# A linear-attention and two-MLP kernel: another order of the second product, weight sums on DVE, later splits for the next tokens, a plain store for the last visit

## The chip, the cores and the metric

The kernel runs on one core of one Trainium2 chip. The metric is the device time of that core in microseconds (us). The kernel before took 1151.75 us, the median of three runs (1151.14 to 1152.44).

The engines are named as in the profile: PE multiplies matrices (PEld is its loading of weights), DVE and ACT do arithmetic and evict PE's accumulators, POOL does arithmetic and issues some DMAs, SP issues most DMAs.

## The reference

```python
kv  = einsum('bhsd,bhse->bhde', k, v)                 # 4 batches, 8 heads, 576 x 64
out = einsum('bhsd,bhde->bhse', q, kv)
x   = out / sqrt(mean(out * out, -1) + 1e-6) * g_norm
x   = x.transpose(0, 2, 1, 3).reshape(2304, 512)
h   = maximum(maximum(x @ w1, x @ w2), x @ w3)        # first MLP, 512 -> 768
x   = h @ w_out                                       # 768 -> 512
p   = domain_probs / (domain_probs.sum(-1) + 1e-9)    # second MLP: 4 experts
for e in range(4):
    h    = maximum(x @ w1[e], 0.0)                    # 512 -> 1024
    out += p[:, e:e+1] * (h @ w2[e])                  # 1024 -> 512
```

All of it is fp32. The change lies in the second MLP, which takes from about 381 us of the span to its end.

## The kernel before

**Numbers and products.** An fp32 operand is split into two fp32r parts, hi and lo: ACT copies the value into hi, which rounds it, and DVE forms lo = value - hi. A product is then three matmuls, hi*hi, lo*hi and hi*lo. On top of that every product of 2x2 blocks is made by seven products of sums of blocks in place of eight products of blocks (Winograd's form of Strassen's method). So a weight matrix goes through three steps before PE can use it: a load by SP, *sums* of its blocks (`w1_sums`, L530, and `w2_sums`, L558, four instructions of 128x256 each, on POOL), and *splits* (`w1_split`, L536 on ACT and L500 on DVE; `w2_split`, L564 and L565), in two halves of 768 and 1024 columns. The tokens y, which are the output of the first MLP, are stored to DRAM as y_d and come back by the same three steps: `y_load`, `y_sum` (L581, four of 128x768, on DVE and POOL in turn) and `y_split` (seven of them, one for each product).

**Visits and units.** The 2304 tokens are three pairs of blocks, sb = 0, 1, 2, of 768 tokens. The hidden columns of the four experts are cut into eight parts, q = 0 to 7 (two for each expert). A visit is one q with one sb; there are 24, in an order in which sb goes 0, 1, 2, then 2, 1, 0, and so on. From visit 0 to 1 and from 1 to 2 the tokens of the next sb are prepared for the first time (**changes of tokens**, the first and the second); their split operands are stored to DRAM by `op_store` and come back ready by `op_load` in all later visits. Each time q advances, at units 6, 12, ... 42, the weights change (**changes of weights**, seven). A visit has two units, r = 0 and 1.

**A unit** is seven slots. In slot k PE makes product k of the first stage (x @ w1 of this visit): six matmuls of 128x384 into bank A or bank X (L604, order AXAXAAX), and then some matmuls of the second stage (h @ w2) of the *previous* visit, 10, 9, 9, 8, 10, 9 and 8 of them, 128x256 each (L855). `after_product` evicts the first stage: product 0 is copied by ACT from bank A into bank X (L658); the additions that read bank X and so free it are on DVE (L645); ReLUs, sums (`relu_sum`, L648; `op_sub`, L694) and splits (`op_hi`, L633 on ACT; `op_lo`, L638 and L640 on DVE) form the operands of the second stage. All but the first steps go through `later(t, ...)`, which puts them into a slot by its number; `at(n, k, ...)` does the same for loads, sums and splits of weights, and `turn_y` for the tokens. Within a slot the order of issue is: product, second stage with its evictions, `later`, `turn_y`, `at`. Each engine works through its own queue in that order.

**The second stage** of a visit is seven products j of 18 matmuls, over three accumulators of two banks each, which rotate from visit to visit. `JACC` gives the accumulator of product j: 0, 2, 1, 0, 2, 0, 0. After product 0 ACT copies accumulator 0 into 1 (L826), so that product 2 adds to it; products 3, 5 and 6 go on in accumulator 0, product 4 in 2. `after_second` evicts products 1, 2, 3, 6 on ACT (L836, scaled by p) and adds products 4 and 5 to them on DVE (L838), each in three instructions. The finished rows of block 0 go out after product 4, those of block 1 after product 6, by `put_out`: a DMA from POOL's queue, which for q > 0 adds to what is in DRAM (`accum_op`). The second stage of the last visit has no unit beside it and stands alone at the end.

## Time and profile before

| | |
|---|---|
| median of three runs | 1151.75 us (1151.14 to 1152.44) |
| the profiled execution | 1152.46 us, its span 1150.7 us |
| mean granted clock of PE | 0.981 |
| PE busy | 1083.1 us, 94% |
| DVE busy | 759.9 us, 66% |
| ACT busy | 595.2 us, 52% |
| POOL busy | 364.8 us, 32% |

A span is what the profiler saw between the first and the last instruction; the time of the execution lies 1.8 us above it. The share of an engine is its busy time by the span, over stages of very different kinds, so the stretches, waits and timelines below are read beside it. "Idle before, releaser" in a row is the time for which the engine stood in front of that work and what it was waiting for at the end.

### The profile page before, as it was taken

The page shows a single profiled execution, that of the slowest core. Times are in us where ns is not written, and L with a number is a line of the kernel's source. Part 1 is how long each engine was busy: PE and PEld are TensorE (multiplying, and loading weights), DVE is VectorE, ACT ScalarE, POOL GpSimd, SP SyncE. Part 2 cuts the span into 40 slices and gives each one's busy share as a digit, 9 for nine tenths or more (in the row PEclk, how much of TensorE's full clock was granted, in tenths as well). Part 3 has the DMA queues.
Part 4 walks back from the last instruction along what each step waited for, and adds up shares of the span by engine and source line. Part 5 has one row for each costly group of instructions (what it writes and reads, how often), then busy time and mean ns, then how long its engine had stood idle before and what let it go on. Part 6 is the DMA issues. An engine that isn't in the chain of part 4 may idle for free.

```text
span 1150.7 us, 19292 instructions
## 1 busy us (share of the span) xinstructions
PE 1083.1 (94%) x7318; PEld 1059.4 (92%) x7318; DVE 759.9 (66%) x1298; ACT 595.2 (52%) x1269; POOL 364.8 (32%) x392
## 2 busy tenths in 40 slices
PE   7889999999999598999999999999999999999995
PEld 6789999999998598999999999999999999999995
DVE  3789985666666866665665675575576476567552
ACT  2543233334344565665565556566556556556553
POOL 1336633420102312512622442341352262253113
PEclk8999999999999898999999999999999999999998
DMA  9945555332412866268668767758858957866855
GB/s 246 295 150 171 154 174 191 128 114 99 133 38 99 312 238 238 93 247 245 131 196 228 173 156 224 208 128 228 237 102 238 282 94 233 231 149 171 230 131 83
DMA packets 109581, 207.61 MB, mean 180 GB/s; under 512 B 13744, under 2 KB 68016, under 8 KB 109488
## 3 DMA queue, kind: packets, MB, share of 16 engines
q1 hardware_dynamic: 88944, 168.29, 43.8%
q0 software_dynamic: 19840, 37.76, 19.1%
q8 instruction: 57, 0.93, 0.3%
q10 hardware_dynamic: 704, 0.33, 0.1%
q14 instruction: 36, 0.29, 0.1%
HBM read 136.35 MB, written 69.99 MB: 179 GB/s over the span
## 4 chain that ended last, share of the span: by engine, by line
PE 49%; DVE 5%; issue 4%; ACT 3%; POOL 1%; POOLq 0%; ACTq 0%; DVEq 0%
PE bank L604 25%; PE bank L855 24%; DVE wl L500 1%; ACT wl L536 1%; DVE ob L838 1%; DVE fa L648 1%; POOL out_dram L813 1%; DVE w2s L838 1%; ACT wr L633 1%; DVE fa L838 1%; ACT fa L836 0%; ACT bank L658 0%; ACT ob L836 0%; DVE fa L645 0%; DVE wr L640 0%
## 5 line engine op out<-in xcount | busy, mean ns | idle before, releaser
L855 PE MATMUL bank<-wr 128*128 128x256 f32 x1683 | 258.5, 284 | 8.9 <-DVE w2s L838 5.1
L855 PEld LDWEIGHTS bank<-wr 128*128 128x128 f32 x1683 | 236.5, 191 | 11.2 <-DVE w2s L838 5.5
L604 PE MATMUL bank<-rb,wl 128*128 128x384 f32 x1032 | 212.0, 341 | 10.6 <-ACT bank L658 10.5
L658 ACT ACTIVATE fa<-bank 128x384 f32<-128x384 f32 x192 | 94.7, 493 | 188.6 <-PE bank L604 181.9
L604 PEld LDWEIGHTS bank<-rb,wl 128*128 128x128 f32 x1032 | 176.6, 189 | 14.1 <-ACT bank L658 12.8
L604 PE MATMUL bank<-xr,wl 128*128 128x384 f32 x864 | 176.4, 339 | 5.9 <-DVE fa L645 4.3
L604 PEld LDWEIGHTS bank<-xr,wl 128*128 128x128 f32 x864 | 146.4, 190 | 7.2 <-DVE fa L645 5.0
L530 POOL TENSOR_TENSOR w1s<-w1s 128x256 f32<-128x256 f32 x96 | 86.8, 924 | 153.3 <-DMA w1s<-in_moe_w_dram 90.5
L640 DVE TENSOR_TENSOR wr<-fa,wr 128x384 fp32r<-128x384 f32 x138 | 83.2, 603 | 56.6 <-ACT wr L633 56.6
L813 POOL DMA_DIRECT2D out_dram<-w2s x49 | 52.3, 1093 | 147.3 <-DVE ob L838 88.5
L855 PE MATMUL bank<-wr,hr 128*128 128x256 f32 x567 | 91.8, 282 | 2.9 <-ACT bank L826 1.4
L813 POOL DMA_DIRECT2D out_dram<-ob x50 | 52.4, 1085 | 128.9 <-DVE fa L838 27.8
L855 PEld LDWEIGHTS bank<-wr,hr 128*128 128x128 f32 x567 | 81.2, 188 | 4.0 <-ACT bank L826 1.6
L633 ACT ACTIVATE wr<-fa 128x384 fp32r<-128x384 f32 x144 | 75.8, 528 | 11.1 <-DVE fa L648 6.6
L813 POOL DMA_DIRECT2D out_dram<-fa x41 | 39.1, 1085 | 106.3 <-DVE fa L838 26.7
L855 PE MATMUL bank<-wr,xr 128*128 128x256 f32 x396 | 68.2, 282 | 1.5 <-DVE w2s L838 1.3
L836 ACT ACTIVATE ob<-bank,p_all 128x256 f32<-128x256 f32 x106 | 50.4, 475 | 30.9 <-PE bank L855 30.9
L645 DVE TENSOR_TENSOR fa<-bank,fa 128x384 f32<-128x384 f32 x96 | 52.9, 551 | 19.6 <-ACT fa L658 17.5
L604 PE MATMUL bank<-op,wl 128*128 128x384 f32 x288 | 60.5, 346 | 5.0 <-ACT fa L658 5.0
L747 DVE TENSOR_TENSOR fa<-bank,fa 128x384 f32<-128x384 f32 x54 | 29.9, 554 | 51.3 <-ACT fa L744 36.0
L836 ACT ACTIVATE w2s<-bank,p_all 128x256 f32<-128x256 f32 x106 | 50.4, 476 | 22.3 <-PE bank L855 22.3
L855 PEld LDWEIGHTS bank<-wr,xr 128*128 128x128 f32 x396 | 58.6, 188 | 2.4 <-DVE w2s L838 1.9
(200 smaller groups left out, 2077.0 us busy)
## 6 DMA issues: line engine op xcount, KB each, us to landing
rb<-op_d SPq DMA_DIRECT2D x42, 768.0 KB, 4.9
xr<-op_d SPq DMA_DIRECT2D x42, 768.0 KB, 9.2
out_dram<-w2s POOLq DMA_DIRECT2D x48, 256.0 KB, 7.7
out_dram<-ob POOLq DMA_DIRECT2D x48, 256.0 KB, 7.1
op<-op_d SPq DMA_DIRECT2D x14, 768.0 KB, 9.7
stage_a<-in_moe_w_dram SPq DMA_DIRECT2D x18, 512.0 KB, 4.1
out_dram<-fa POOLq DMA_DIRECT2D x32, 256.0 KB, 7.9
w1s<-in_moe_w_dram SPq DMA_DIRECT2D x30, 256.0 KB, 3.7
```

Of the source, the lines that this page charges most:

```text
L500: nc.vector.tensor_tensor(out=lo, in0=src, in1=f32(hi), op=ALU.subtract)
L530: eng.tensor_tensor(out=st[o], in0=st[a], in1=st[b], op=ALU.subtract)
L604: nc.tensor.matmul(out, w[wi][:, c * P : (c + 1) * P], y[yi][:, c, :], start=(i == 0 and k in begin), stop=(i == 5), skip_group_check=k no ...
L633: nc.scalar.activation(out=ops[key][0], in_=src, func=AF.Relu if relu else AF.Copy)
L640: nc.vector.tensor_tensor(out=lo, in0=src, in1=f32(hi), op=ALU.subtract)
L645: todo.setdefault(t, []).append(lambda: fn(*args, **kw))
L658: nc.scalar.activation(out=out, in_=in_, func=func)
L747: nc.vector.tensor_tensor(out=mx[done] if i == 0 else t, in0=x, in1=t, op=ALU.add)
L813: nc.gpsimd.dma_start(out=rows, in_=src, accum_op=ALU.add)
L836: nc.scalar.activation(out=o, in_=piece(ps, i), func=AF.Copy, scale=pe)
L838: nc.vector.scalar_tensor_tensor(out=o, in0=piece(ps, i), scalar=pe, in1=o, op0=ALU.mult, op1=ALU.add)
L855: nc.tensor.matmul(piece(ps, i), h[hi][:, i * P : (i + 1) * P], w[wi], start=fresh, stop=last, skip_group_check=True,)
```

## The change

Four things are changed, all in the second MLP:

- The second stage goes through its products in the order 0, 1, 3, 2, 5, 4, 6. The accumulators of `JACC` stay, so that no two products in a row use the same one (0, 2, 0, 1, 0, 2, 0). Product 3 now takes the place of product 2 as the one that opens the rows of block 0.
- All sums of w1, w2 and y are on DVE. They are spread over slots, two instructions in each, and stand in other slots than before. Loads of w2 are called in an earlier slot; on SP's queue they stand in the same place among the other DMAs as before.
- At the two changes of tokens y is summed in slots 0 to 3 and split from slot 3 on (`YLAG`), in place of slots 0 and 1 for the sums and 0 to 6 for the splits. The addition that frees bank X after product 6 is made at once and not through `later`, and the splits of S1, S2 and A12 stand in another order.
- The last visit's rows are loaded back from DRAM into `fa` during the last unit (`get_out`); all its evictions add to them on DVE, and `put_out` stores them plainly from SP's queue.

```diff
--- before.py
+++ after.py
@@ -524,9 +524,9 @@
             src = e_w1[e, :, f * P : (f + 1) * P].rearrange("(c p) f -> p c f", p=P)
             nc.sync.dma_start(out=st[:, at : at + 2].rearrange("p n c f -> p (n c) f"), in_=src)
 
-    def w1_sums(eng, early=False):
+    def w1_sums(eng, early=False, which=(0, 1, 2, 3)):
         st = [t[:, n * 2 * P : (n + 1) * 2 * P] for t in w1_at(early) for n in range(4)]
-        for o, a, b in ((4, 0, 2), (5, 1, 4), (6, 1, 0), (7, 3, 5)):
+        for o, a, b in [((4, 0, 2), (5, 1, 4), (6, 1, 0), (7, 3, 5))[x] for x in which]:
             eng.tensor_tensor(out=st[o], in0=st[a], in1=st[b], op=ALU.subtract)
 
     def w1_split(r, half, early=False):
@@ -551,11 +551,12 @@
                 out=st[:, x : y + 1 : y - x, :], in_=e_w2[e, f * P : (f + 1) * P, :].rearrange("p (n d) -> p n d", n=2)
             )
 
-    def w2_sums(q, r):
+    def w2_sums(q, r, which=(0, 1, 2, 3)):
         t = w2_at(q, r)
         st = [t[:, n * 2 * P : (n + 1) * 2 * P] for n in range(8)]
-        for o, a, b, op in ((1, 7, 0, ALU.subtract), (3, 1, 4, ALU.subtract), (5, 4, 7, ALU.subtract), (6, 2, 3, ALU.add)):
-            nc.gpsimd.tensor_tensor(out=st[o], in0=st[a], in1=st[b], op=op)
+        sums = ((1, 7, 0, ALU.subtract), (3, 1, 4, ALU.subtract), (5, 4, 7, ALU.subtract), (6, 2, 3, ALU.add))
+        for o, a, b, op in [sums[x] for x in which]:
+            nc.vector.tensor_tensor(out=st[o], in0=st[a], in1=st[b], op=op)
 
     def w2_split(q, r, half):
         cols = slice(0, 3 * 2 * P) if half == 0 else slice(3 * 2 * P, 7 * 2 * P)
@@ -676,14 +677,14 @@
             later(t0 + 7, op_hi, key("S1"), u)
             later(t0 + 7, op_lo, key("S1"), u)
             later(t0 + 11, nc.vector.tensor_tensor, out=r21, in0=r11, in1=r21, op=ALU.subtract)
-            later(t0 + 8, op_sub, n, r11, u)
+            later(t0 + 7, op_sub, n, r11, u)
         elif k == 6:
-            later(t0 + 6, nc.vector.tensor_tensor, out=t12, in0=x, in1=t12, op=ALU.add)
+            nc.vector.tensor_tensor(out=t12, in0=x, in1=t12, op=ALU.add)
+            later(t0 + 8, op_hi, key("S2"), u)
             later(t0 + 8, op_hi, key("A12"), t12, True)
+            later(t0 + 9, op_lo, key("S2"), u)
             later(t0 + 9, op_lo, key("A12"), t12, True)
             later(t0 + 10, relu_sum, t12, t12, u, ALU.add)
-            later(t0 + 9, op_hi, key("S2"), u)
-            later(t0 + 10, op_lo, key("S2"), u)
             later(t0 + 11, op_hi, key("S4"), t12)
             later(t0 + 12, op_lo, key("S4"), t12)
             later(t0 + 12, op_hi, key("S3"), r21)
@@ -793,6 +794,7 @@
     ACC = [banks[0:2], banks[2:4], banks[4:6]]
     JOPS = ["A11", "S1", "A12", "S2", "S4", "S3", "A22"]
     JACC = (0, 2, 1, 0, 2, 0, 0)
+    YLAG = 3
     ev_turn = [0]
 
     def new_ev(q):
@@ -804,12 +806,21 @@
     def piece(acc, i):
         return acc[i // 2][:, i % 2 * 2 * P : (i % 2 + 1) * 2 * P]
 
-    def put_out(q, sb, blk, ev, i):
+    def get_out(sb, blk, i):
+        t = (2 * sb + blk) * TPB + i
+        n = P // len(tiles[t])
+        held[blk, i, 1] = part(fa, (blk * TPB + i) * DM, DM)
+        for x, rows in enumerate(tiles[t]):
+            nc.sync.dma_start(out=held[blk, i, 1][x * n : (x + 1) * n, :], in_=rows)
+
+    def put_out(gi, q, sb, blk, ev, i):
         t = (2 * sb + blk) * TPB + i
         n = P // len(tiles[t])
         for x, rows in enumerate(tiles[t]):
             src = ev[x * n : (x + 1) * n, :]
-            if q:
+            if gi + 1 == len(visits):
+                nc.sync.dma_start(out=rows, in_=src)
+            elif q:
                 nc.gpsimd.dma_start(out=rows, in_=src, accum_op=ALU.add)
             else:
                 nc.gpsimd.dma_start(out=rows, in_=src)
@@ -827,22 +838,22 @@
             return
         blk, b = {1: (1, 1), 2: (0, 0), 3: (0, 1), 4: (0, 1), 5: (1, 1), 6: (1, 0)}[j]
         for i in (0, 1) if half == 0 else (2,):
-            if j in (1, 2):
+            if j in (1, 3) and gi + 1 < len(visits):
                 held[blk, i] = new_ev(q)
-            ev = held[blk, i]
+            ev = held[(blk, i) if gi + 1 < len(visits) else (blk, i, 1)]
             pe = p_all[:, (2 * sb + blk) * TPB + i, e : e + 1]
             o = ev[:, b * 2 * P : (b + 1) * 2 * P]
-            if j in (1, 2, 3, 6):
+            if j in (1, 2, 3, 6) and gi + 1 < len(visits):
                 nc.scalar.activation(out=o, in_=piece(ps, i), func=AF.Copy, scale=pe)
             else:
                 nc.vector.scalar_tensor_tensor(out=o, in0=piece(ps, i), scalar=pe, in1=o, op0=ALU.mult, op1=ALU.add)
             if j in (4, 6):
-                put_out(q, sb, blk, ev, i)
+                put_out(gi, q, sb, blk, ev, i)
 
     def second(gi, q, sb):
 
         acc = [ACC[(gi + x) % 3] for x in range(3)]
-        for j in range(7):
+        for j in (0, 1, 3, 2, 5, 4, 6):
             ps = acc[JACC[j]]
             for half, its in enumerate(((0, 1), (2,))):
                 fresh = j in (0, 1)
@@ -1121,45 +1132,45 @@
             at(0, 2 + i, w1_split, 1, i)
             at(0, 5 + i, w2_split, 0, 0, i)
         at(0, 0, w2_load, 0, 0)
-        at(0, 1, w2_sums, 0, 0)
+        at(0, 4, w2_sums, 0, 0)
         at(1, 0, w2_load, 0, 1)
-        at(1, 1, w2_sums, 0, 1)
-        at(1, 5, w2_split, 0, 1, 0)
-        at(2, 1, w2_split, 0, 1, 1)
+        at(1, 5, w2_sums, 0, 1)
+        at(1, 6, w2_split, 0, 1, 0)
+        at(2, 2, w2_split, 0, 1, 1)
         for k in range(7):
             at(0, (0, 1, 2, 3, 5, 5, 5)[k], op_store, 0, k)
-            at(2, k, op_store, 1, k)
-            at(4, k, op_store, 2, k)
+            for sb in range(1, NSB):
+                at(2 * sb - 1, k + YLAG, y_split, k)
+                at(2 * sb, k, op_store, sb, k)
+        for sb in range(1, NSB):
+            for i in range(4):
+                at(2 * sb - 1, i, y_sum, nc.vector, i)
+        at(0, 4, y_load, 1)
+        at(2, 5, y_load, 2)
         for q in range(1, Q):
             e, pr, n = q // 2, q % 2 * 2, 6 * q
             at(n - 2, 0, w1_load, e, pr)
-            at(n - 2, 1, w1_sums, nc.gpsimd)
-            at(n - 1, 1, w1_split, 0, 0)
-            at(n - 1, 3, w1_split, 0, 1)
             at(n - 1, 5, w1_load, e, pr + 1)
-            at(n - 1, 6, w1_sums, nc.gpsimd)
-            at(n, 3, w1_split, 1, 0)
-            at(n, 5, w1_split, 1, 1)
+            for i in range(2):
+                which = (2 * i, 2 * i + 1)
+                at(n - 2, 5 + i, w1_sums, nc.vector, False, which)
+                at(n, 2 + i, w1_sums, nc.vector, False, which)
+                at(n - 1, 1 + 2 * i, w1_split, 0, i)
+                at(n, 4 + i, w1_split, 1, i)
+                for r in range(2):
+                    at(n - 1 + r, 4 + i, w2_sums, q, r, which)
+                    at(n + 1 + i, (0, 3)[r], w2_split, q, r, i)
             for r in range(2):
-                at(n - 1 + r, 4, w2_load, q, r)
-                at(n - 1 + r, 5, w2_sums, q, r)
-                at(n + 1, (0, 3)[r], w2_split, q, r, 0)
-                at(n + 2, (0, 3)[r], w2_split, q, r, 1)
+                at(n - 2 + r, 6, w2_load, q, r)
+        last = len(visits) - 1
+        for blk in range(2):
+            for i in range(TPB):
+                at(2 * last + 1, i, get_out, visits[last][1], blk, i)
 
         def turn_y(gi, r, k):
 
             (q, sb), (_, nxt) = visits[gi], visits[gi + 1]
-            if sb == nxt:
-                return
-            if q == 0:
-                if r == 0 and k == (4 if gi == 0 else 1):
-                    y_load(nxt)
-                if r == 1 and k < 2:
-                    for i in range(2):
-                        y_sum(nc.gpsimd if i else nc.vector, 2 * k + i)
-                if r == 1:
-                    y_split(k)
-            elif r == 1:
+            if q and r == 1 and sb != nxt:
                 op_load(nxt, k)
 
         fill = second_of(*units[-1][:2])
```

PE at the end of a second stage (here that of the last visit; bank4_70 and bank5_71 are accumulator 0, bank2_68 and bank3_69 accumulator 2; wr_957 holds the weights and the other names the operands). Before, products 4, 5 and 6:

```order
L855 MATMUL bank2_68<-wr_957 128x256 x6
L855 MATMUL bank2_68<-wr_957,xr_81 128x256 x6
L855 MATMUL bank3_69<-wr_957 128x256 x3
L855 MATMUL bank3_69<-wr_957,xr_81 128x256 x3
L855 MATMUL bank4_70<-wr_957,xr_81 128x256 x6
L855 MATMUL bank4_70<-wr_957,rb_1097 128x256 x6
L855 MATMUL bank5_71<-wr_957,xr_81 128x256 x3
L855 MATMUL bank5_71<-wr_957,rb_1097 128x256 x3
L855 MATMUL bank4_70<-wr_957 128x256 x6
L855 MATMUL bank4_70<-wr_957,hr_82 128x256 x6
L855 MATMUL bank5_71<-wr_957 128x256 x3
L855 MATMUL bank5_71<-wr_957,hr_82 128x256 x3
```

and now products 5, 4 and 6:

```order
L866 MATMUL bank4_70<-wr_957 128x256 x6
L866 MATMUL bank4_70<-wr_957,xr_81 128x256 x6
L866 MATMUL bank5_71<-wr_957 128x256 x3
L866 MATMUL bank5_71<-wr_957,xr_81 128x256 x3
L866 MATMUL bank2_68<-wr_957,rb_1097 128x256 x6
L866 MATMUL bank2_68<-wr_957 128x256 x6
L866 MATMUL bank3_69<-wr_957,rb_1097 128x256 x3
L866 MATMUL bank3_69<-wr_957 128x256 x3
L866 MATMUL bank4_70<-wr_957 128x256 x12
L866 MATMUL bank5_71<-wr_957 128x256 x6
```

Products 5 and 6, which stood one behind the other on accumulator 0, now have product 4 between them.

DVE at the first change of tokens, in unit 1 (L581, now L582, are sums of y, L694/L695 is `op_sub`, L500 with rb or xr a split of y, L645/L646 with bank6 an addition that frees bank X, L638 to L641 are splits of the second stage's operands, L559 are sums of w2). Before:

```order
L581 TENSOR_TENSOR fa_80<-fa_80 128x768
L500 TENSOR_TENSOR rb_1097<-fa_80,rb_1097 128x768
L694 TENSOR_TENSOR fa_80<-fa_80 128x384
L581 TENSOR_TENSOR fa_80<-fa_80 128x768
L500 TENSOR_TENSOR rb_1097<-fa_80,rb_1097 128x768
L638 SCALAR_TENSOR_TENSOR wr_957<-fa_80,wr_957 128x384
L640 TENSOR_TENSOR wr_957<-fa_80,wr_957 128x384
L500 TENSOR_TENSOR rb_1097<-fa_80,rb_1097 128x768
L648 SCALAR_TENSOR_TENSOR fa_80<-fa_80 128x384
L640 TENSOR_TENSOR wr_957<-fa_80,wr_957 128x384
L500 TENSOR_TENSOR xr_81<-fa_80,xr_81 128x768
L645 TENSOR_TENSOR fa_80<-fa_80 128x384
```

and now:

```order
L695 TENSOR_TENSOR fa_80<-fa_80 128x384
L582 TENSOR_TENSOR fa_80<-fa_80 128x768 x2
L641 TENSOR_TENSOR wr_957<-fa_80,wr_957 128x384
L639 SCALAR_TENSOR_TENSOR wr_957<-fa_80,wr_957 128x384
L641 TENSOR_TENSOR wr_957<-fa_80,wr_957 128x384
L582 TENSOR_TENSOR fa_80<-fa_80 128x768
L649 SCALAR_TENSOR_TENSOR fa_80<-fa_80 128x384
L582 TENSOR_TENSOR fa_80<-fa_80 128x768
L500 TENSOR_TENSOR rb_1097<-fa_80,rb_1097 128x768
L646 TENSOR_TENSOR fa_80<-fa_80 128x384
L646 TENSOR_TENSOR fa_80<-bank6_72,fa_80 128x384
L500 TENSOR_TENSOR rb_1097<-fa_80,rb_1097 128x768
```

All four sums of y stand on DVE, and the first split of y comes behind them, next to the addition that frees bank X and not six instructions ahead of it.

DVE at the second change of weights, in unit 12 (L500 with w1s is a split of w1, L559 with fa are sums of w2). Before:

```order
L500 TENSOR_TENSOR wl_83<-w1s_1626,wl_83 128x768
L645 TENSOR_TENSOR fa_80<-fa_80 128x384
L645 TENSOR_TENSOR fa_80<-bank6_72,fa_80 128x384
L640 TENSOR_TENSOR wr_957<-fa_80,wr_957 128x384
L500 TENSOR_TENSOR wl_83<-w1s_1626,wl_83 128x1024
L640 TENSOR_TENSOR wl_83<-fa_80,wl_83 128x384
L648 SCALAR_TENSOR_TENSOR fa_80<-fa_80 128x384
L645 TENSOR_TENSOR fa_80<-bank6_72,fa_80 128x384
```

and now:

```order
L646 TENSOR_TENSOR fa_80<-fa_80 128x384
L646 TENSOR_TENSOR fa_80<-bank6_72,fa_80 128x384
L500 TENSOR_TENSOR wl_83<-w1s_1626,wl_83 128x768
L559 TENSOR_TENSOR fa_80<-fa_80 128x256 x2
L641 TENSOR_TENSOR xr_81<-fa_80,xr_81 128x384
L500 TENSOR_TENSOR wl_83<-w1s_1626,wl_83 128x1024
L559 TENSOR_TENSOR fa_80<-fa_80 128x256 x2
L682 TENSOR_TENSOR fa_80<-bank6_72,fa_80 128x384
```

The addition that frees bank X (bank6_72, L646) now stands ahead of the split of 768 columns; two pairs of sums came in, and L682, the addition after product 6, stands directly behind the second pair.

## Rows read from the trace of the kernel before

**Rows 1.** Busy time by stretch: length, PE, PEld, DVE, ACT, POOL, granted clock, DMA, GB/s.

```profile
395.00:408.00 13.00, 8.47 (x30) 7.87 (x31) 12.75 (x18) 5.85 (x11) 4.17 (x5) 0.52 0.43 142
...
436.00:443.00 7.00, 6.75 (x30) 6.75 (x31) 5.22 (x10) 2.15 (x5) 0.00 (x0) 0.60 0.87 353
...
462.00:1122.00 660.00, 643.44 (x4484) 637.31 (x4483) 418.38 (x745) 384.37 (x862) 221.53 (x251) 1.00 0.70 190
```

**Rows 2.** Waits of PE from 462 to 1141 us: us in total, times, longest.

```profile
PE bank L604 <- ACT bank L658: 7.3, 7, 1.3
...
PE bank L855 <- DVE w2s L838: 3.6, 8, 0.8
...
PE bank L855 <- DVE ob L838: 3.1, 8, 0.8
...
PE bank L855 <- DVE fa L838: 2.8, 7, 0.8
...
PE bank L855 <- ACT bank L826: 1.4, 1, 1.4
```

**Rows 3.** Timeline of PE, changes of tokens: start, us, work, idle before, releaser.

```profile
395.23 2.29 PE L604 MATMUL bank<-op,wl 128*128 128x384 f32 x6 [4.97 <-ACT fa L658]
...
401.82 2.29 PE L604 MATMUL bank<-xr,wl 128*128 128x384 f32 x6 [4.30 <-DVE fa L645]
...
408.11 1.22 PE L604 MATMUL bank<-rb,wl 128*128 128x384 f32 x6
...
436.25 0.58 PE L855 MATMUL bank<-wr 128*128 128x256 f32 x1 [4.79 <-DVE w2s L838]
```

**Rows 4.** Timeline of DVE and POOL, first change of tokens.

```profile
387.80 0.96 DVE L581 TENSOR_TENSOR fa<-fa 128x768 f32<-128x768 f32 x1 [2.38 <-DMA fa<-y_d]
...
389.54 2.17 DVE L694 TENSOR_TENSOR fa<-fa 128x384 f32<-128x384 f32 x1
...
393.38 2.16 DVE L638 SCALAR_TENSOR_TENSOR wr<-fa,wr 128x384 fp32r<-128x384 f32 x1
...
395.46 1.10 DVE L640 TENSOR_TENSOR wr<-fa,wr 128x384 fp32r<-128x384 f32 x1
...
399.88 0.95 DVE L500 TENSOR_TENSOR xr<-fa,xr 128x768 fp32r<-128x768 f32 x1
...
401.22 0.55 DVE L645 TENSOR_TENSOR fa<-bank,fa 128x384 f32<-128x384 f32 x1
...
388.89 2.41 POOL L581 TENSOR_TENSOR fa<-fa 128x768 f32<-128x768 f32 x1 [21.98 <-ACT fa L658]
...
395.41 4.13 POOL L558 TENSOR_TENSOR ob<-ob 128x256 f32<-128x256 f32 x4 [0.29 <-DMA ob<-in_moe_w_dram]
```

**Rows 5.** Timeline of DVE and PE at the second change of weights.

```profile
581.91 1.23 DVE L500 TENSOR_TENSOR wl<-w1s,wl 128x1024 fp32r<-128x1024 f32 x1 [2.29 <-ACT wl L536]
...
583.99 0.55 DVE L645 TENSOR_TENSOR fa<-bank,fa 128x384 f32<-128x384 f32 x1
...
585.16 1.32 PE L604 MATMUL bank<-rb,wl 128*128 128x384 f32 x6 [0.95 <-ACT bank L658]
```

**Rows 6.** Timeline of POOL and ACT, two units earlier.

```profile
550.70 3.45 POOL L530 TENSOR_TENSOR w1s<-w1s 128x256 f32<-128x256 f32 x4 [7.28 <-DMA w1s<-in_moe_w_dram]
...
552.19 0.47 ACT L658 ACTIVATE bank<-bank 128x384 f32<-128x384 f32 x1 [1.68 <-DVE hr L638]
```

**Rows 7.** Timeline of PE and POOL at the end.

```profile
1139.43 0.52 PE L855 MATMUL bank<-wr,hr 128*128 128x256 f32 x3
...
1144.20 0.90 POOL L813 DMA_DIRECT2D out_dram<-fa  x1 [0.46 <-issue]
```

**Rows 8.** Groups by line, DVE: busy us, mean ns, idle before, releaser.

```profile
L838 DVE SCALAR_TENSOR_TENSOR w2s<-bank,p_all,w2s 128x256 f32<-128x256 f32 x53 | 25.3, 477 | 9.9 <-PE bank L855 9.8
```

**Rows 9.** DMA issues from 360 to 445 us: count, KB each, median us to landing.

```profile
y_d<-fa SPq DMA_DIRECT2D x6, 192.0 KB, 3.5
...
y_d<-ob SPq DMA_DIRECT2D x2, 192.0 KB, 1.9
```

## Prediction

> **What bounds the kernel now.** I read the table of stretches first, then PE's waits, then the timelines at the places where PE stood. From 462 to 1122 us PE is busy 643.4 of 660 us at the full clock of 2.4 GHz [rows 1]: that stage is 97.5% full, and only the missing 16.6 us are to be had there. Outside it two places are poor. At the first change of tokens (visit 0 to 1) PE stood 4.97 and 4.30 us, and from 395 to 408 us the granted clock was 0.52, the 1.2 GHz level; at the second (visit 1 to 2) it stood 4.79 us, and the clock of the next 7 us was 0.60 [rows 1, 3]. At the end the last matmuls finish by 1139.95 us, while the span goes on to 1150.7 us for POOL's last accumulating stores [rows 7].
>
> What PE waited for in the full stage and the tail is in its list of waits. DVE's evictions of the second product (L838) come to 3.6 + 3.1 + 2.8 = 9.5 us in 23 waits [rows 2], one for each visit, since product 6 writes the banks that product 5 has just filled; the 4.79 us are one more of them. ACT's copy of bank A into bank X (L658) is 7.3 us in 7 waits [rows 2], one at each change of weights, as at 585.16 [rows 5].
>
> **The change, part by part.**
>
> *Order of the second product.* Between products 5 and 6 now stands product 4, on other banks: 18 matmuls and at least one product of the next visit's first stage, 24 matmuls of 0.143 us on average (643.4 us by 4484) [rows 1], 3.4 us. In that time DVE has three evictions of 0.477 us to do [rows 8]. So the 23 waits go: **-9.5 us**. No pair in the new order is closer than one that was there already: product 3 follows product 1 and needs ACT's copy of product 0, which product 2 needed at the same place; product 5 has one product between it and product 3, as before. Block 0 is stored one product later, on POOL, for which nobody waits.
>
> *Sums on DVE.* 56 sums of w1 and 64 of w2, each 128x256, go from POOL to DVE. The trace has none on DVE. Undisturbed, a 128x768 and a 128x384 instruction take 1.34 us from 399.88 to 401.22 [rows 4]; I count 0.87 and 0.47 (their 0.95 and 0.55 less the 0.08 that lies under the next), so 1.04 ns a column and 0.34 us for 256. 120 x 0.34 = 41 us go onto DVE; 112 of them lie in the stretch where DVE is busy 418 of 660 us [rows 1], which becomes 456, 69%. They are spread two by two over slots of 15 matmuls, 2.1 us, so what counts is who is queued behind them. **Bank X.** Before, between the split of the weights (ends 583.14) and the addition that frees bank X (583.99) stand two instructions [rows 5]; now two sums stand there (0.68 us) and the addition comes first behind them: it starts 0.2 to 0.3 us earlier, and PE's wait of 0.95 us shrinks by as much. Seven times: **-2 us**. Bounds: the waits go wholly (-7), or a sum costs as much as on POOL, 1.03 us [rows 4], and the wait grows by 1.1 us at each change (+8). I take the value from DVE's own rows.
>
> *The wait that is new.* The sums of w1 wait for their load, now on DVE. At the second change of weights the load landed at 550.70, as POOL's start shows, and the copy that PE waits for ran at 552.19 [rows 6]. Behind the waiting sums stands the addition for bank X: 550.70 + 0.68 + 0.55 = 551.93, so 0.26 us are left. SP's order there is as before, and its transfers too, so I take the landing as it is: **+1 us** over the six changes where POOL waited so, for loads that land a little later against a faster PE; bounds 0 and +6 (each landing 1.3 us later).
>
> *First change of tokens.* DVE's instructions there were held up by POOL: two of 384 columns took 2.17 and 2.16 us where an undisturbed one takes 0.55, and four from 395.46 to 399.88 took 4.42 us instead of 2.28, 5.4 us in all, while POOL did two sums of y (2.41 us the first) and four of w2 [rows 4]. Those six now cost DVE 2 x 0.87 + 4 x 0.34 = 3.1 us. Second, y_split is put off by three slots, so that ACT and DVE come to the instructions that free banks A and X before most of the splits. I count DVE's new order from 387.80 on, where it still waits for the load of y: eleven instructions up to the addition that frees bank X make 7.2 us, so product 6 starts at about 395.0 and not at 401.8, with one stop of some 5 us in place of 4.97 + 4.30; eleven more up to the first split of w2's second half make 5.9 us, and that half is ready at 401. The second product of visit 0 needs it after six matmuls, so product 1 of the next unit starts near 401.3 where it started at 408.11 [rows 3]: 6.8 us. A stop of 5 us left the clock at its lower level before, so I give back 2: **-5 us**, bounds -2 and -9. The Trainium skill ("SBUF — State Buffer", Who interferes with whom) has DVE instructions with two SBUF inputs and GpSimd instructions that read SBUF lock each other out for whole instructions. By that rule this term would be -8 (rival E); the rows agree in kind, but the four sums of 4.13 us cost DVE only 2.1.
>
> *Second change of tokens.* The 4.79 us are the pair 5 and 6, which is gone; the clock's 7 us at 0.60 cost 2.8. DVE's work in that unit, 13 instructions of 0.47, six evictions of 0.4, four sums of y and four splits of 0.87, is about 15.5 us, as long as the 7 slots of 2.1 us that PE takes for it; I allow 0.5 us: **-7 us**, bounds -3 and -7.6.
>
> *The end.* The last visit's outputs come back by SP during the last unit, into a part of fa that nothing uses any more; DVE adds to them from PSUM, three evictions for each product of 18 matmuls (1.4 against 2.6 us). After the last matmul (1139.95, less 0.3 for the pair 5 and 6) come an eviction of 0.48 [rows 8], 0.6 us that I allow for hand-over and issue, and a plain store of 256 KB. No such store is in the trace; stores of 192 KB to y_d landed in 1.9 and 3.5 us [rows 9]. I take 2.7: end near 1143.5 in place of 1150.7, **-7 us**, bounds -5 and -8. The splits of S2, A12 and S3 in another order cost nothing: each is issued at least one slot ahead of its use.
>
> **Sum**: -9.5 - 2 + 1 - 5 - 7 - 7 = -29.5 us. The profiled execution took 1152.46 us (span 1150.7); that gives 1123. It lies 0.7 us above the median of the runs, so 1122 to 1123 for a median; I say **1123**.
>
> **The rivals.** *B, DVE becomes the bound where it was already late.* At the first change of tokens DVE has no idle time from 387.80 on [rows 4]; all sums now stand in its one queue, so the first change may gain nothing, the second only part. With the first at 0, the second at -3 and bank X at 0: -9.5 + 1 - 3 - 7 = -18.5, 1134. Against it: the 5.4 us that POOL took are more than the 3.1 that it hands over. The Trainium skill ("Trace Analysis", Optimizing Scalar/DVE Operations) speaks against the change here: work may be moved off a saturated DVE to Scalar or GpSimd; it adds that GpSimd and DVE share a port, so that it might not help. *C, the pair's wait moves.* In the tail PE waited 1.4 us for ACT's copy of product 0 (L826) [rows 2]. If product 3, now behind product 1, waited 0.5 us for it in each of 23 visits, the order would gain nothing: 1123 + 12 = 1135. For it: the copy must now be past its reading. Against it: product 2 needed the copy at the same place, and the list has that wait once. *D, slower.* DVE stands still for a w1 load that lands late at six changes; each us beyond the 0.26 us of slack costs PE one. The point is a landing 5.3 us later ((5.3 - 0.26) x 6 = 30); 6 us later gives 1123 - 1 + 34 = 1156. For it: 0.26 us is little, and POOL had waited 7.28 us there [rows 6]. Against it: the transfers ahead are the same. *E, better.* POOL's sums held DVE up for as long as they ran, 2 x 2.4 + 4.1 = 9 us [rows 4], and bank X is free in time: -9.5 - 7 + 1 - 8 - 7.6 - 7 = -38, 1114.
>
> **How the numbers follow.** Forecast 0.62, B 0.17, C 0.07, E 0.09, D 0.05. Forecast, B and C lie between 1116 and 1138 with their bounds; leaving out D, half of E and the far ends gives 1113 to 1138. A measurement of this kernel tells about 0.2% (2.3 us) from no change. Faster is all but D and mixtures of D with the rest: 0.92; same 0.03, slower 0.05.
>
> **What would show it.** In the profile after: no wait of PE for an eviction in each visit; PE's waits for ACT's copy at the changes of weights between 0.5 and 0.8 us; sums of 128x256 on DVE near 0.42 us long; product 6 at the first change of tokens near 395 and one stop in place of two; the second stop gone with its low clock; the span's end within 4 us of the last matmul. DVE idle before w1 sums with PE waiting behind it would show D; stops of PE behind DVE from 385 to 440 us as long as before, B. What would most easily make it wrong is the first change of tokens, where I counted a queue by hand.

## The result, and the profile after

| | before | after |
|---|---|---|
| median | 1151.45 us (4 runs) | 1130.76 us (1130.14 to 1131.67, 4 runs) |
| profiled execution, its span | 1152.46 us, 1150.7 us | 1131.67 us, 1129.9 us |
| DVE busy | 759.9 us, 66% | 768.4 us, 68% |
| POOL busy | 364.8 us, 32% | 236.1 us, 21% |

The ratio of the times is 0.9821, with a 95% interval of 0.9804 to 0.9838: 20.7 us less. The prediction said 1123, 28.8 us below the 1151.75 that were known then, and 1113 to 1138. The direction and the range hold; somewhat over a quarter of the forecast gain is missing. The stretches of [rows 1] in the changed kernel (same columns):

```profile
395.00:408.00 13.00, 11.91 (x79) 11.65 (x78) 11.10 (x20) 10.65 (x20) 0.00 (x0) 0.96 0.75 291
436.00:443.00 7.00, 7.00 (x52) 7.00 (x51) 5.86 (x11) 5.01 (x12) 0.00 (x0) 1.00 1.01 387
462.00:1122.00 660.00, 643.39 (x4506) 639.13 (x4505) 425.76 (x851) 382.44 (x858) 119.51 (x141) 1.00 0.71 190
```

The two poor stretches at the changes of tokens are nearly full. The windows lie at the same times and hold later work than before, though: the one long stop that is left at the first change ends at 392.17 us, ahead of the first of them. By the marks explained below, the granted clock went from 0.82 to 0.90 over the first change and from 0.85 to 1.00 over the second. In the full stage PE is busy no longer than it was, 643.39 against 643.44 of 660 us, and makes only 22 matmuls more in that time, about 3 us of work. Its list of waits from 462 us on (us in total, times, longest) says why; it answers to [rows 2]:

```profile
PE bank L866 <- DVE wr L566: 6.1, 7, 0.9
PE bank L605 <- ACT bank L659: 5.4, 7, 1.0
PE bank L605 <- DVE fa L646: 3.0, 6, 0.5
PE bank L866 <- ACT bank L837: 2.1, 1, 2.1
```

The 23 waits for DVE's evictions, 9.5 us, are gone. Two kinds of wait stand there that were not there before: for DVE's split of w2 (L566), once for each change of weights, and for the addition that frees bank X after product 4 (L646), once in the unit ahead of each.

**Where the time went, by stages.** Each unit has exactly one copy of bank A into bank X, which ACT makes after product 0. The starts of these copies are marks by which two traces can be laid side by side; the difference of two marks is the length of a unit, or of several.

| from mark to mark | before | after | gain | forecast |
|---|---|---|---|---|
| start to unit 1 | 383.12 | 380.10 | 3.0 | 0 |
| units 1 and 2 (first change of tokens) | 38.84 | 34.39 | 4.5 | 5 |
| unit 3 (second change of tokens) | 22.77 | 16.70 | 6.1 | 7 |
| units 4 to 46 | 663.73 | 660.64 | 3.1 | 10.5 |
| unit 47 to the end of the span | 42.24 | 38.07 | 4.2 | 7 |

The 3.0 us at the start don't belong to the change. The run with only the new order, whose code up to there is that of before, reached the mark at 381.50. The profiled execution of before had a granted clock of 0.63 from 367 to 371 us; from mark 0 to mark 1 it took 17.61 us, every other kernel of this study 16.04 to 16.09, with the first sums of w2 on either engine. The other 1.4 us are in mark 0 itself, which lies anywhere from 363.55 to 365.74 us in the kernels of this study. So what failed is above all the term of units 4 to 46, and there the unit two behind each change of weights tells most, in which the second product meets the new weights for the first time. Marks of units 14 and 15 before:

```profile
599.69 0.47 ACT L658 ACTIVATE bank<-bank 128x384 f32<-128x384 f32 x1
614.60 0.47 ACT L658 ACTIVATE bank<-bank 128x384 f32<-128x384 f32 x1 [1.68 <-PE bank L604]
```

and after:

```profile
584.40 0.47 ACT L659 ACTIVATE bank<-bank 128x384 f32<-128x384 f32 x1 [0.15 <-PE bank L605]
600.49 0.47 ACT L659 ACTIVATE bank<-bank 128x384 f32<-128x384 f32 x1 [1.66 <-PE bank L605]
```

14.91 us became 16.09, and likewise behind each of the seven changes of weights. The timeline of that unit in the changed kernel:

```profile
591.90 0.48 ACT L847 ACTIVATE w2s<-bank,p_all 128x256 f32<-128x256 f32 x1
592.26 1.07 ACT L565 ACTIVATE wr<-fa 128x1024 fp32r<-128x1024 f32 x1
...
593.36 1.23 DVE L566 TENSOR_TENSOR wr<-fa,wr 128x1024 fp32r<-128x1024 f32 x1 [2.63 <-ACT wr L565]
...
594.64 0.63 PE L866 MATMUL bank<-wr,wl 128*128 128x256 f32 x3 [0.87 <-DVE wr L566]
```

ACT's and DVE's split of the second half of w2 (products 3 to 6) for the second unit stand in slot 3, behind ACT's evictions of product 1. The old order needed that half after 54 matmuls, the new one takes product 3 after 36, and PE stands until the split is made.

### The profile page after: what moved, and what is told of

It reads as the page before. It is cut to its first block, busy times and chain, and to the rows that moved or that the text cites. A ratio compares the mean times of both kernels' runs of the same rounds, so it can differ in the third digit from the quotient of the medians.

```text
span 1129.9 us, 19220 instructions
## 1 busy us (share of the span) xinstructions
PE 1078.0 (95%) x7318; PEld 1056.9 (94%) x7318; DVE 768.4 (68%) x1434; ACT 591.7 (52%) x1257; POOL 236.1 (21%) x261
## 4 chain that ended last, share of the span: by engine, by line
PE 59%; DVE 16%; DMA 8%; issue 7%; ACT 7%; SPq 1%; POOL 1%; DVEq 0%; ACTq 0%; POOLq 0%
PE bank L605 33%; PE bank L866 21%; PE bank L772 4%; DMA w_da<-cv_a 1%; PE bank L424 1%; DMA w1s<-in_moe_w_dram 1%; DMA y_d<-fa 1%; DMA out_dram<-ob 1%; DMA out_dram<-w2s 1%; DVE wr L566 1%; DVE wl L500 1%; ACT wl L536 1%; ACT ob L847 1%; DVE rb L500 1%; DVE cv_a L233 1%
## 5 line engine op out<-in xcount | busy, mean ns | idle before, releaser
L866 PE MATMUL bank<-wr 128*128 128x256 f32 x1701 | 263.6, 283 | 5.0 <-DVE wr L566 2.8
L866 PEld LDWEIGHTS bank<-wr 128*128 128x128 f32 x1701 | 239.5, 190 | 5.8 <-DVE wr L566 3.4
L641 DVE TENSOR_TENSOR wr<-fa,wr 128x384 fp32r<-128x384 f32 x131 | 72.3, 552 | 47.8 <-ACT wr L634 47.6
L824 POOL DMA_DIRECT2D out_dram<-w2s x48 | 48.5, 1037 | 200.1 <-DVE ob L849 152.0
L824 POOL DMA_DIRECT2D out_dram<-ob x48 | 48.0, 1038 | 173.2 <-DVE w2s L849 93.2
L634 ACT ACTIVATE wr<-fa 128x384 fp32r<-128x384 f32 x152 | 78.4, 529 | 5.2 <-DVE fa L646 2.4
L748 DVE TENSOR_TENSOR fa<-bank,fa 128x384 f32<-128x384 f32 x54 | 29.9, 554 | 51.6 <-ACT fa L745 36.3
L824 POOL DMA_DIRECT2D out_dram<-fa x37 | 34.2, 1053 | 128.8 <-DVE fa L849 72.0
L530 POOL TENSOR_TENSOR w1s<-w1s 128x256 f32<-128x256 f32 x40 | 35.2, 898 | 110.2 <-DMA w1s<-in_moe_w_dram 48.9
L682 DVE TENSOR_TENSOR fa<-bank,fa 128x384 f32<-128x384 f32 x48 | 26.6, 554 | 43.6 <-PE bank L605 43.5
```

The lines of the kernel that those rows point to most:

```text
L530: eng.tensor_tensor(out=st[o], in0=st[a], in1=st[b], op=ALU.subtract)
L634: nc.scalar.activation(out=ops[key][0], in_=src, func=AF.Relu if relu else AF.Copy)
L641: nc.vector.tensor_tensor(out=lo, in0=src, in1=f32(hi), op=ALU.subtract)
L682: nc.vector.tensor_tensor(out=t12, in0=x, in1=t12, op=ALU.add)
L748: nc.vector.tensor_tensor(out=mx[done] if i == 0 else t, in0=x, in1=t, op=ALU.add)
L824: nc.gpsimd.dma_start(out=rows, in_=src, accum_op=ALU.add)
```

## Experiments

All but one start from the changed kernel (1130.8 us) and undo or move one thing.

**The split of w2 one slot earlier.**

```diff
-                    at(n + 1 + i, (0, 3)[r], w2_split, q, r, i)
+                    at(n + 1 + i, (0, 3 - i)[r], w2_split, q, r, i)
```

> The changed kernel, with the second half of w2's second unit split one slot earlier (slot 2 of the unit in which the new second product begins, in place of slot 3). Theory (due time): the new order takes product 3 in place of product 2, so its weights, which lie in the second half, are due 18 matmuls earlier; the split stayed where it was. Then PE's 7 waits for DVE's split of w2 (6.1 us) go, and with them the 0.3 us by which each of those units was longer than its wait explains: 8 us, 1122.5 to 1124.5. Rival (DVE too full of sums): the split comes late because of what is queued ahead of it on DVE, so an earlier place wins little: the waits stay above 3 us and the time above 1128.

Measured: 1123.31 us, ratio to before 0.9755 (0.9742 to 0.9767). The wait has left the list, and the marks of units 14 and 15 are

```profile
583.56 0.47 ACT L659 ACTIVATE bank<-bank 128x384 f32<-128x384 f32 x1 [0.16 <-PE bank L605]
598.46 0.47 ACT L659 ACTIVATE bank<-bank 128x384 f32<-128x384 f32 x1 [1.67 <-PE bank L605]
```

14.90 us. From mark 4 to mark 47 it is 652.44 us, 8.2 less than after. The wait was a matter of due time, and DVE had room for the split.

**The order alone, and everything but the order.** The first is the kernel before with the two lines below, the second the changed kernel without them.

```diff
-        for j in range(7):
+        for j in (0, 1, 3, 2, 5, 4, 6):
...
-            if j in (1, 2):
+            if j in (1, 3):
```

> The kernel before with nothing changed but the order of the second product (0, 1, 3, 2, 5, 4, 6; product 3 opens the rows of block 0). Theory (due time): the 23 waits for product 5's evictions go, 7 waits of 0.7 to 1.0 us for the split of w2 come, with the sums still on POOL: 3 to 5 us less than before, 1146.5 to 1148.5. Rival (the split is late only because of the sums on DVE): no such waits, 10 to 12 us less than before, 1139.5 to 1141.5.

> The changed kernel with the second product in the old order 0 to 6, everything else as changed. Theory (due time): PE's 23 waits for the evictions of product 5 come back (9.5 us; 11 to 12 by the length of the units), and the 7 waits for w2's split go (6.1 us; 8 by the length of the units): 1132 to 1136, and no wait for the split of w2 in the list. Rival (DVE too full): the waits for the split of w2 stay, and the pairs come on top: 1140 to 1143.

Measured: 1144.8 us (ratio 0.9947, 0.9933 to 0.996) and 1138.95 us (0.9894, 0.9881 to 0.9906). The list of waits of the order alone, from 440 us on:

```profile
PE bank L855 <- DVE wr L565: 6.1, 7, 0.9
PE bank L604 <- ACT bank L658: 5.7, 7, 1.0
...
```

and of everything but the order:

```profile
PE bank L866 <- DVE w2s L849: 5.6, 8, 1.7
...
PE bank L866 <- DVE ob L849: 4.5, 8, 1.6
PE bank L866 <- DVE fa L849: 4.1, 7, 1.4
...
```

The wait for the split comes with the order, with the sums still on POOL, to the tenth of a microsecond. Both times lie beside what I wrote, and on the same side: the order gained 6 us where I expected 3 to 5, and to take it out cost 8 where I expected 1 to 5. The order was worth more than the 9.5 us that the pairs have in the list of before. From mark 4 to 47, where 21 of the 23 pairs lie, the old order with everything else takes 665.98 us, the new order without the late split 652.44: 13.5 us. The same from the side of before: 663.73 - 657.65, and 8.2 for the late split, is 14.3. From the side of the changed kernel two things make up the difference. With everything else changed, the pairs themselves come to 14.2 us in the list and no longer to 9.5, the longest 1.7 instead of 0.8 us, while the 3.5 us of waits for L646 are not there. And PE's own busy time between these marks, for the same number of matmuls, falls from 647.15 to 643.57 us.

**S2 back in its slots.**

```diff
-            later(t0 + 8, op_hi, key("S2"), u)
             later(t0 + 8, op_hi, key("A12"), t12, True)
-            later(t0 + 9, op_lo, key("S2"), u)
+            later(t0 + 9, op_hi, key("S2"), u)
             later(t0 + 9, op_lo, key("A12"), t12, True)
+            later(t0 + 10, op_lo, key("S2"), u)
```

> The changed kernel with the split of operand S2 back in its old slots (hi one slot later, behind that of A12; lo one slot later). Theory (an ACT instruction in front of the split of w1): with both hi splits in one slot, ACT comes to the first split of w1 0.5 us later in the unit before each change of weights, DVE behind it too, and its addition that frees bank X comes after product 6 wanted to start; those 6 waits of 0.5 us make the unit 15.6 us long where it was 14.7 with the old placement. So the unit falls to 14.7 to 15.0 and the time by 4.5 to 6.5 us: 1124.5 to 1126.5, and S2 is still in time for product 3. Rival (the sums on DVE make that unit long): no wait goes, time within 1 us of the changed kernel's 1130.8; or S2 comes too late for product 3 and the time rises.

Measured: 1124.82 us (ratio 0.9768, 0.9753 to 0.9783). The unit ahead of each change of weights fell from 15.64 to 14.97 us, and the waits for L646 left the list. The timeline of unit 11 in the changed kernel:

```profile
541.25 0.53 ACT L634 ACTIVATE hr<-fa 128x384 fp32r<-128x384 f32 x1
541.68 0.51 ACT L634 ACTIVATE wr<-fa 128x384 fp32r<-128x384 f32 x1
542.09 0.83 ACT L536 ACTIVATE wl<-w1s 128x768 fp32r<-128x768 f32 x1
...
542.95 0.96 DVE L500 TENSOR_TENSOR wl<-w1s,wl 128x768 fp32r<-128x768 f32 x1 [1.74 <-ACT wl L536]
...
549.66 0.55 DVE L646 TENSOR_TENSOR fa<-bank,fa 128x384 f32<-128x384 f32 x1
...
550.26 1.31 PE L605 MATMUL bank<-xr,wl 128*128 128x384 f32 x6 [0.46 <-DVE fa L646]
```

and with S2 back:

```profile
540.45 0.52 ACT L634 ACTIVATE hr<-fa 128x384 fp32r<-128x384 f32 x1
...
540.86 0.85 ACT L536 ACTIVATE wl<-w1s 128x768 fp32r<-128x768 f32 x1
...
541.74 0.96 DVE L500 TENSOR_TENSOR wl<-w1s,wl 128x768 fp32r<-128x768 f32 x1 [1.07 <-ACT wl L536]
...
548.44 0.56 DVE L646 TENSOR_TENSOR fa<-bank,fa 128x384 f32<-128x384 f32 x1
...
549.05 1.31 PE L605 MATMUL bank<-xr,wl 128*128 128x384 f32 x6
```

One split of 0.5 us more stands on ACT ahead of the split of w1 in the first. Counted from the mark of the unit (537.97 and 537.44 us), DVE begins its split of w1 after 4.98 us in the first and after 4.30 in the second. From there on DVE has no idle time; twelve instructions stand between this split and the addition that frees bank X, and the 0.68 us arrive there in full: it starts 11.69 and 11.00 us behind the mark.

**The later sums of w1 and w2 on POOL.** Each of these sums is issued in its new slot, with POOL in place of DVE.

> The changed kernel with all sums of w1 and w2 from the first change of weights on back on POOL, in their new slots (the sums of the first visit and of y stay on DVE). Theory: DVE then has fewer instructions but is held up by POOL's; the unit of each change of weights goes from 16.25 to 16.5 us, that two units ahead from 14.9 to 15.2, and the unit just ahead stays at 15.6, since its wait comes from the place of S2: 3 to 4 us more, 1134 to 1135. Rival (the sums on DVE make the unit just ahead of the change long): that unit falls to 14.7, and the time is 2 to 4 us below the changed kernel, 1127 to 1129.

Measured: 1127.43 us (ratio 0.9789, 0.9774 to 0.9804), 3.3 us faster than the changed kernel; I had expected 3 to 4 us slower. The unit ahead of the change of weights stayed at 15.65, as the theory had it. The unit of the change itself did not grow to 16.5: it fell from 16.25 to 15.58. The list from 440 us on:

```profile
...
PE bank L605 <- DVE fa L646: 3.5, 7, 0.5
...
PE bank L605 <- ACT bank L659: 0.4, 1, 0.4
```

In the changed kernel two sums stand on DVE between the split of w1 and the addition that frees bank X (L682):

```profile
568.56 0.75 DVE L559 TENSOR_TENSOR fa<-fa 128x256 f32<-128x256 f32 x2
569.23 0.55 DVE L682 TENSOR_TENSOR fa<-bank,fa 128x384 f32<-128x384 f32 x1
...
570.40 1.32 PE L605 MATMUL bank<-rb,wl 128*128 128x384 f32 x6 [0.76 <-ACT bank L659]
```

Their 0.7 us are the whole wait. POOL does hold DVE up in this run:

```profile
550.89 4.63 POOL L559 TENSOR_TENSOR fa<-fa 128x256 f32<-128x256 f32 x4
...
552.82 1.09 DVE L649 SCALAR_TENSOR_TENSOR fa<-fa 128x384 f32<-128x384 f32 x1
...
553.83 1.09 DVE L639 SCALAR_TENSOR_TENSOR wr<-fa,wr 128x384 fp32r<-128x384 f32 x1
```

DVE's instructions of 0.55 us take 1.09 beside it, but that lies where DVE has room. From mark 4 to 47 DVE is busy 438.9 us, 7.7 us longer than in the changed kernel (431.3), although 112 sums of 0.42 us have left it: what stayed on DVE took over 50 us longer. The Trainium skill ("SBUF — State Buffer", Who interferes with whom) has a DVE instruction with two SBUF inputs and a GpSimd instruction that reads SBUF contend for a shared port, as an exclusive lock; the rows agree that DVE is held up, and the time says that this costs nothing where nobody waits for DVE. The advice that spoke against the change in the prediction, from the Trainium skill ("Perfetto Trace Analysis", Optimizing Scalar/DVE Operations), is that work may be moved off a saturated DVE, with the proviso that between DVE and GpSimd it might not help. DVE was not saturated here, and its busy time agrees with the proviso; the 3.3 us came from the place of two sums, not from DVE's load.

**The first sums of w2 on POOL, and the sums of y.** The first run gives POOL the sums of unit 0, in slot 1; the second gives it two of the four sums of y at each change of tokens.

> The changed kernel with the first four sums of w2 (first unit of the first visit) back on POOL and in their old slot 1. Theory (POOL holds DVE up): DVE's two splits of 128x384 that stand beside these sums take about 2.1 us together in place of 1.0, PE's wait behind them grows by 0.4 us, the clock drops there, and the first unit of the second MLP takes 2 to 3 us more: 1133 to 1134. Rival: the 3 us that the changed kernel was ahead there came from the loads at the start of the program, which differ from run to run: 1130 to 1131.5, and DVE's splits as short as in the changed kernel.

> The changed kernel with two of the four sums of y at each change of tokens back on POOL; the later splits stay. Theory (POOL holds DVE up): two sums of 0.9 us leave DVE, but what runs on DVE beside POOL's 2.4 us takes 1.5 us longer each time, so the stop of 4.8 us at the first change is no shorter, 0 to 1.5 us more at each of the two changes: 1131 to 1133.5. Rival (DVE is the bound there by its own work, and POOL beside it would be a help): each stop shortens by about 1 us, 1128.5 to 1129.5.

Measured: 1132.6 us (0.9841, 0.9827 to 0.9856) and 1132.01 us (0.9827, 0.9814 to 0.9841); neither differs clearly from 1130.8. In unit 0 two splits on DVE beside POOL's sums:

```profile
362.95 2.08 DVE L500 TENSOR_TENSOR hr<-fa,hr 128x384 fp32r<-128x384 f32 x2
```

They took 1.02 us in the changed kernel, as the theory had it, and PE's stop behind them was 1.97 us in place of 1.50. The rest of the theory did not come: the clock did not fall behind that stop as it had in the trace of before, and the first unit took 16.05 us in both. The trace is that of the fastest of the four executions (1130.44; the others took 1132.42 to 1134.03), so it does not show whether the clock fell in the others. With two sums of y on POOL the first change of tokens took 34.33 us against 34.39, the second 17.25 against 16.70. The long stop at the first change was 3.9 us in place of 4.8, as the rival had it, and still the time did not fall; the granted clock of unit 1 was 0.71 in place of 0.81.

**The old slots of y.** `YLAG = 0`, the sums in slots 0 and 1, all still on DVE.

> The changed kernel with y summed in slots 0 and 1 and split from slot 0 on, as before, but all of the sums on DVE. Theory (the later splits are what gains at the changes of tokens): the splits stand again ahead of the additions that free bank X; the second stop at the first change comes back (3 to 5 us) and some of the one at the second change (1 to 3 us): 1134 to 1139. Rival (POOL's sums held DVE up, and taking them off it is what gained, as my prediction's term has it for 2.3 of its 6.8 us and its rival E for more): at most 2 us more, 1130 to 1133.

Measured: 1138.76 us (ratio 0.9893, 0.9867 to 0.9919), 8.0 us slower, as the theory had it in sum, of which the marks show 6.3; but the place is another than I wrote. The first change of tokens takes 35.13 us in place of 34.39, and the second 21.55 in place of 16.70, by one stop of PE:

```profile
431.77 2.29 PE L605 MATMUL bank<-xr,wl 128*128 128x384 f32 x6 [3.61 <-DVE fa L646]
```

Units 4 and 6 lose another 0.7 us.

**Later splits beside POOL's sums.** The sums of y on POOL as above, and beside them the second unit's sums of w2 of the first visit on POOL, in slot 1; the splits stay in their later slots.

> The changed kernel with the later splits of y, but at the first change of tokens POOL has all that it had before: two of the sums of y (at both changes), and the second unit's first sums of w2 in slot 1. With old splits and all sums on DVE the two units of the first change take 35.1 us, with old splits and POOL's sums 38.8, with later splits and DVE's sums 34.4. Theory A (either part alone is enough, since each takes what stood ahead of the addition that frees bank X): 34.4 to 35.5 us here, and 1131 to 1133 in all. Theory B (POOL beside DVE is what cost the 4.4 us): 37 to 39 us here, and 1134 to 1136.

Measured: 1137.35 us (ratio 0.988, 0.9852 to 0.9909); units 1 and 2 took 40.06 us. That is past theory B's time, but not cleanly its mechanism:

```profile
394.19 3.96 POOL L559 TENSOR_TENSOR ob<-ob 128x256 f32<-128x256 f32 x4 [37.43 <-DMA ob<-in_moe_w_dram]
...
398.12 4.31 POOL L582 TENSOR_TENSOR fa<-fa 128x768 f32<-128x768 f32 x2
...
398.70 2.06 DVE L500 TENSOR_TENSOR rb<-fa,rb 128x768 fp32r<-128x768 f32 x1
...
400.69 2.17 DVE L641 TENSOR_TENSOR wr<-fa,wr 128x384 fp32r<-128x384 f32 x1
```

POOL waited for the load of w2 with the sums of y queued behind it, which the kernel before didn't do; so the run mixes POOL's hold on DVE with a queue that I made myself.

**The end as before.**

> The changed kernel with the end as before: the last visit's rows evicted by ACT and DVE in turn and stored by POOL's accumulating DMAs. My prediction's term says 7 us more, 1137 to 1138.5. By the traces as far as read, the time from the last unit's mark to the end is 42.2 to 43.5 us with the old end and 36.3 to 38.1 with the new one: 5 to 6 us, 1135.5 to 1137. A rival by which the stores are hidden anyway would give no more than 2 us.

Measured: 1139.95 us (ratio 0.9895, 0.9881 to 0.9909), 9.2 us more, past both of the figures that I gave. From mark 47 to the end of the span it is 44.96 us against 38.07, so the new end is worth 6.9 us in this pair, as the term had it. Another 1.7 us lie ahead of mark 1, where the edit changes nothing.

**All mends together.** The earlier split of w2 and S2 back in its slots; at the end ACT's copy ahead of the splits of S3 and S4, and the last stores from SP and ACT; and the second unit's sums of w2 either behind the addition (slot 6 and the next 0, on DVE) or on POOL.

> The changed kernel with the mends that the runs point to: the second half of w2 for the second unit split a slot earlier (8.1 us), S2's split back in its old slots (5 us), the second unit's sums of w2 two slots later, behind the addition that frees bank X, still on DVE (7 waits of 0.76 us: 4.7 us); at the end ACT's copy of accumulator 0 ahead of the splits of S3 and S4 (PE's wait of 2.1 us and what the clock loses behind it, 2 to 3.5 us), and the last stores from two queues (0.5 us). If the gains add up: 1130.8 - 8.1 - 5 - 4.7 - 3 - 0.5 = 1109.5, within 1108 to 1113. Rival (DVE full: each mend moves the wait on): above 1115, with a new wait for DVE in the list, once for each change of weights.

> The same, but the second unit's sums of w2 stay in their slots and go to POOL. If what cost bank X time was only that these sums stood ahead of the addition on DVE, this is as good as putting them behind it: within 1.5 us of the other kernel. Rival (POOL holds DVE up): the unit of each change of weights is 0.3 us longer than in the other, 2 us in all.

Measured: 1110.75 us (ratio 0.9655, 0.9631 to 0.9679) and 1112.48 us (0.9665, 0.964 to 0.9689). The gains add up to 20.0 us where I had 21.3, and from mark 4 to 47 the two take 643.03 and 643.39 us, so the rival's 2 us for POOL's hold on DVE are not there. From mark 47 on the first takes 34.30 us where the changed kernel took 38.07. All of that lies ahead of the last matmul. The second queue for the last stores brought nothing: the span ends 5.5 us behind the last matmul, against 5.2 to 5.4 with one queue. From 384 us on this is the whole list of PE's waits in the first of them:

```profile
PE bank L605 <- ACT fa L659: 6.5, 2, 4.7
PE bank L605 <- DVE fa L646: 1.1, 1, 1.1
PE bank L866 <- DVE wr L566: 1.1, 1, 1.1
PE bank L605 <- ACT bank L659: 0.4, 1, 0.4
```

The first and the third line lie at the first change of tokens, the second at the second, and the last at one change of weights. This version is 20 us faster than the changed kernel and 39 to 41 faster than before.

## Why the prediction was right or wrong

*Order of the second product, -9.5.* The waits went, as written, and with them about 14 us. The step that failed is the sentence that no pair in the new order is closer than one that was there already. It looked at accumulators alone. The weights have due times as well: product 3 was moved 18 matmuls ahead, the split of its half of w2 was not, and that cost 8.2 us, shown by moving the split. So the term was -6 and not -9.5. My rival C had the right form (a new wait in the place of the pair, for an operand of product 3) and named the wrong operand.

*The splits of S2 and A12, 0.* "Each is issued at least one slot ahead of its use" was true of these splits and said nothing of what they are put in front of. Seven waits, 4.8 us from mark 4 to 47 (660.64 - 655.87), shown by putting S2 back.

*Bank X, -2.* Right in size: units of the change of weights went from 16.52 to 16.25, seven times 0.27 is 1.9 us, and the waits are 0.70 to 1.04 us long, where I had 0.5 to 0.8. But the sums that I counted as cheaper than what had stood there are all of what is left, 4.7 us (660.64 - 655.91).

*The wait for w1's load, +1.* It did not cost anything: DVE stood 15.7 us in front of these sums, but PE had no wait in these units, and from the second change of weights on the units two ahead of it took 14.9 us where they had taken 14.9 to 15.6. D never came near. Together the four terms are -14 + 8.2 + 4.8 - 1.9 = -2.9; the marks say -3.1.

*First change of tokens, -5.* Measured -4.5. PE's stops there after the change:

```profile
392.17 2.29 PE L605 MATMUL bank<-op,wl 128*128 128x384 f32 x6 [4.83 <-ACT fa L659]
...
399.56 0.61 PE L866 MATMUL bank<-wr 128*128 128x256 f32 x3 [1.09 <-DVE wr L566]
```

One stop of some 5 us is left of two, as [rows 3] and the count of DVE's queue gave it. The count was too short: product 6 starts 14.2 us behind mark 1 where it had started 18.7 behind it, and I had counted 11.9. Which part did it is only half shown. The order alone did not: it left both stops, 4.8 and 4.4 us, and 38.76 us for the two units. With all sums on DVE the old splits cost 0.7 us, so the later splits are not needed here; two sums of y on POOL cost nothing either. That leaves the sums of w2 in slot 1 on POOL, or several of these parts together; no run moved them cleanly by themselves, so this cause stays open. Rival B is out; so is the -8 of rival E.

*Second change, -7.* Measured -6.1, for a reason that the term named only in part. It put the whole gain down to the pair 5 and 6. The order alone, which takes the pair away, gained 1.9 us (20.86 us for unit 3 against 22.77), because PE then stood nearly as long for the addition that frees bank X:

```profile
435.89 1.96 PE L604 MATMUL bank<-xr,wl 128*128 128x384 f32 x6 [3.88 <-DVE fa L645]
```

Everything but the order gained 3.6 us (19.14). The other part is the later splits: without them 4.85 us come back, with the new order in place. My count of DVE's work had them in it, as four splits in the unit and not seven, but I had not given them a share. Of the stops 1.1 us are left, where I had allowed 0.5.

*The end, -7.* The profiled pair shows -4.2; undoing the end in the changed kernel shows +6.9 behind mark 47. The two differ in what the new end is compared with. With the order alone the old end takes 43.55 us from mark 47 where it had taken 42.24, and 13.1 us from the last matmul where it had taken 10.7: block 0 is stored one product later (the first of its stores is issued 28.8 us behind the mark and not 27.0), on POOL, for which I had written that nobody waits. At the end the kernel does. The rest is the stop told next, which undoing the end leaves as it is. What the profiled pair lacks of its 7 us is in two things. The first lies ahead of the last matmul:

```profile
1110.92 0.52 ACT L634 ACTIVATE xr<-fa 128x384 fp32r<-128x384 f32 x1
1111.35 0.85 ACT L837 ACTIVATE bank<-bank 128x512 f32<-128x512 f32 x2
...
1111.98 1.03 PE L866 MATMUL bank<-wr 128*128 128x256 f32 x6 [2.10 <-ACT bank L837]
```

PE's stop before product 3 is 2.1 us where it was 1.4 [rows 2], because ACT splits S4 and S3 first, and behind it the granted clock was 0.72 for 4 us; in another run of the same code at the end it stayed at 1.00, and the end took 36.3 us. With S2 back in its slots the stop is 1.5 us, the clock stays at 1.00, and the end takes 35.8 us. The second lies behind the last matmul, where 5.4 us come and not 3.8:

```profile
1122.16 4.38 SPq L822 DMA_DIRECT2D out_dram<-fa  x7
...
1123.81 1.27 DVE L849 SCALAR_TENSOR_TENSOR fa<-bank,p_all,fa 128x256 f32<-128x256 f32 x3 [0.89 <-PE bank L866]
```

I counted one eviction and one store; it is three evictions and, of the seven issues above, the last four one behind the other on one queue, in 2.2 us. The last store is issued 1.5 us behind the last matmul, where I had 1.1, and lands after 2.5 us, where I took 2.7. The rest of the difference is 1.3 us from that landing to the end of the span, which I had left out.

*The sum.* Forecast -29.5 against a profiled execution. Measured between the profiled spans: -20.8, of which 3.0 lie ahead of anything that was changed. Two costs that the sum had at nothing make most of the shortfall, the late split of w2 (8.2 us) and the place of S2 (4.8); the order's own gain, larger by 4.5 us than its waits in the list, made up for a part.

## What to carry to other kernels

When an order of products is changed, each of their operands has a due time: the accumulator, the left operand, the weights, and what prepares each. Go through all of them, and not only through the one for which the order is changed. A step moved to an earlier slot stands in front of something; follow that queue to the next engine that waits, even where the step itself has room. And two sums of together 0.7 us cost their full length on an engine that is 65% busy if they stand ahead of the one instruction that frees a bank, and nothing two slots later. Last, a wait that goes can uncover another close behind it: at the second change of tokens the new order alone changed a stop of 4.8 us for one of 3.9.

## What the runs showed of the hardware

A wait of PE can cost more than its row in the list says: 0.87 us of waiting made a unit 1.14 to 1.19 us longer, 8.2 us for 6.1 in seven waits, and 3.5 us in seven other waits were worth 4.8. In both cases PE's busy time between marks 4 and 47 fell as well when the waits went, from 645.63 to 643.57 and 644.37 us, for the same number of matmuls. It is no rule: the seven waits for bank X went from 5.4 to 0.4 us and were worth 4.7, with PE's busy time as it was (645.60). Why the first two kinds cost more is open.

DVE's instructions took twice their time beside POOL's sums (1.09 for 0.55), and four such sums took about three times as long on POOL beside DVE's work as on DVE (4.63 us against 1.54); the fastest single one on POOL took 0.73 us, against 0.42 on DVE.

The clock after a stop is not the same in each execution: after 1.9 to 2.1 us without matmuls the granted clock fell towards the 1.2 GHz level in some profiles (before from 367 us, 0.63 for 4 us; after at the end, 0.72 for 4 us) and stayed at 2.4 GHz in another (the first sums of w2 on POOL, behind stops of 1.97 us at the same place and 2.10 us at the end).
